# First units of a fused mLSTM and mixture-of-experts kernel: another order of the first loads, and a gate move in two transfers instead of three

## The chip, the cores and the metric

The kernel runs on one core of one Trainium2 chip. The metric is device time in microseconds, the median of several executions of the whole program.

## The reference

Four sequences of 768 steps with 8 heads of 40 go through a gated recurrence with a matrix memory; its output, 3072 tokens of 320, goes through a top-2 mixture of 8 experts. Cut to what matters:

```python
m_new  = np.maximum(f_gate[:, :, t] + m, i_gate[:, :, t])
f_stab = np.exp(f_gate[:, :, t] + m - m_new)
i_stab = np.exp(i_gate[:, :, t] - m_new)
C = f_stab * C + i_stab * outer(vt, kt)
n = f_stab * n + i_stab * kt
y[:, :, t] = sigmoid(o_gate) * (C @ qt) / np.maximum(abs(n @ qt), 1.0)
# then, on x = y as [3072, 320]:
noisy = x @ w_gate + noise * np.log1p(np.exp(x @ w_noise))
# top 2 of 8 experts, softmax over the two
out[mask] += top2_w * (np.maximum(x[mask] @ w1[e], 0) @ w2[e])
```

## The kernel before, in words

The recurrence is done in chunks of 64 steps. A **unit** is one chunk for one half of the batch (two sequences on the two partition halves, 8 heads); there are 24 units, 12 for each half. Four buffers rotate: unit u uses QK[u % 4] (queries and keys by feature) and VKS[u % 4] (values, keys by time, and the output gates). The mixture of experts follows in the second and longer part of the kernel, and its routing begins beside the units.

The schedule is manual: each engine works in the order in which the program issues instructions to it, and waits where an operand that another engine or a transfer writes isn't there. All loads of the first stretch go through SP's queue, in program order too; an issue that waits holds back the issues behind it.

What a unit does, by name:

- `load_unit(u, "k")` is two transfers of queries and keys (160 KB each, 40 partitions each) into QK; `load_unit(u, "v")` is two of 242 KB into VKS. Before a QK buffer is loaded its rows 32 to 63 and 96 to 127 are zeroed by `blank(i, engine)`.
- `gate_math` is eight VectorE instructions over 64 partitions that turn the gates of some steps (tile `raw`, loaded from `fi_in`, in several pieces) into the two rows of HL. `gate_move(kk)` carries the part of HL for two units into the operand tiles LE[kk % 2] and RE[kk % 2]: one transfer into LE (32 rows) and two into RE (row 96 and row 97, each gathered from 16 rows). Before unit 0, gate moves 0 and 1 go through SP's queue; later ones through GpSimd's queue, from iteration 13 on through SP's again.
- `operands` and `heads` fill the constant parts of LE and RE (ScalarE and VectorE).
- `e_part(u)` is one matmul for each half from LE and RE, and an exponential on ScalarE: the decay matrix W[u] (L308, L311).
- `s_part(u)` is the query-key products, 32 matmuls (L333), and for a unit that isn't a sequence's first, two longer ones per half with the identity `ident` as an operand (L329), which is in the first 128 columns of the constants `cs`.
- `k_part(u)` (VectorE, L341) multiplies `VKS[u % 4][:, :, 328:648]`, all 128 partitions of both halves, by a column of W[u], and gives KD[u]. `p_part(u)` (L347, L351 for a first unit) multiplies the products by W[u] and gives PP[u].
- `c_part(u)` (32 matmuls L361) forms the state from KD[u], and ScalarE copies it into VK[(u + 1) % 4] (L364). `o_part(u)` (32 matmuls L370) forms the output from PP[u]. `f_part` divides by the denominator and multiplies by the output gate (VectorE, then GpSimd L382).
- `keys(i)` prepares rows of VK[i] that no load writes: two zeroings (L244, L245) and two copies of `ident` (L246, L247), on GpSimd. Columns 328 to 648 of these rows lie in what `k_part` reads. In unit 0 `c_part` and `o_part` use only the loaded rows (`kr`).

Before the loop over units the program issues on TensorE: 16 warm-up matmuls on zeros (`WARM`), `s_part(0)`, 12 more (`WARM2`), `e_part(0)`, `s_part(1)`, `e_part(1)`. On VectorE behind the gate math of units 0 to 3 come `heads(1, 0)`, `k_part(0)`, `p_part(0)`, then `gate_math(256, 384)` and four further steps of gate math. Iteration i of the loop then has, on TensorE, `c_part(i)`, `o_part(i)`, half of `e_part(i+2)`, `s_part(i+2)`, the other half of `e_part(i+2)`; on VectorE `k_part(i+1)`, `p_part(i+1)`, `f_part(i)` and steps of gate math or routing; a gate move in every second iteration, two iterations ahead of its first use.

The order in which SP's queue gets the first loads is: gates of steps 0 to 127, constants `cet`, queries of unit 0, `ident`, gates 128 to 255, values of unit 0, gate move 0, queries and values of unit 1, gates 256 to 511, queries of unit 2, gate move 1, the rest of the gates, values of unit 2. GpSimd's is: `blank(1)`, `blank(2)`, `keys(0)`, `keys(1)`, `blank(3)`, `keys(2)`, `keys(3)`.

Of the kernel before, what the change touches and what calls it, by code (L numbers as in the profile page):

```python
# [7 lines left out]
F32 = mybir.dt.float32  # L8
# [28 lines left out]
NB = 4  # L37

STEP, SHARE = 0.19, 1.65
WARM, WARM2 = 16, 12  # L40
LEAD = 2
TURN = 6
OR1 = (0, 6, 1, 2, 3, 4, 5)
# [15 lines left out]
def build(ctx, tc, qk, vk, fi, noise, wgn, w1, w2, cst, ce, out):  # L59
    nc = tc.nc  # L60
    V, A, P, T, SP = nc.vector, nc.scalar, nc.gpsimd, nc.tensor, nc.sync
# [10 lines left out]
    cs = keep.tile([128, C_END], F32, name="cs")  # L72
# [24 lines left out]
    RE = [gates.tile([128, 2, H, GC * L], FR, name=f"re{i}") for i in range(2)]  # L97
# [53 lines left out]
    def load_unit(u, what="kv", q=None):  # L151
        pr, c = divmod(u, NCH)
        if "k" in what:
            for p in range(2):
                (q or SP).dma_start(QK[u % 4][64 * p:64 * p + D], qk[pr, c, p])
        if "v" in what:
            flat = VKS[u % 4].rearrange("p x c -> p (x c)")
            SP.dma_start(flat[0:64, 0:VW], vk[pr, c, 0])
            SP.dma_start(flat[64:128, 648:648 + VW], vk[pr, c, 1])
# [3 lines left out]
    fit = raw[0:64, 0:2 * S].rearrange("p (x t) -> p x t", x=2)  # L163
# [8 lines left out]
    def blank(i, q):  # L172
        q.memset(QK[i][32:64], 0.0)
        q.memset(QK[i][96:128], 0.0)
# [6 lines left out]
    V.memset(rmt[:, 0:256], 1.0)  # L181
    V.memset(rmt[:, 0:256].rearrange("p (c t) -> p c t", t=L)[:, :, 0], 0.0)
    load_unit(0, "k")
    SP.dma_start(cs[:, 0:128], cst[:, 0:128])
    SP.dma_start(fit[:, :, 128:256], fi[:, :, 128:256])
    load_unit(0, "v")

    def run(steps):
        for _ in steps:
            pass  # L190

    def gate_math(t0, t1):
        f, i = fit[:, 0, t0:t1], fit[:, 1, t0:t1]
        n = t1 - t0
        V.tensor_tensor_scan(mt[:, t0 + 1:t1 + 1], f, i, mt[:, t0:t0 + 1], OP.add, OP.max)
        yield
        gt = gts[t0 // 128 % 2][:, 0:n]
        V.tensor_add(gt, f, mt[:, t0:t1])
        yield
        V.tensor_sub(gt, gt, mt[:, t0 + 1:t1 + 1])  # L200
        if t0 == 0:
            V.memset(gt[:, 0:1], 0.0)
        yield
        ag = ags[t0 // 128 % 2][:, :, 0:n]
        V.tensor_tensor_scan(ag[:, 1, :], rmt[:, 0:n], gt, 0.0, OP.mult, OP.add)
        yield
        V.tensor_sub(ag[:, 0, :], i, mt[:, t0 + 1:t1 + 1])
        yield
        V.tensor_sub(ag[:, 0, :], ag[:, 0, :], ag[:, 1, :])
        yield  # L210

        V.tensor_copy(HL[:, :, t0:t1], ag)
        yield
        V.scalar_tensor_tensor(HL[:, :, t0:t1], HL[:, :, t0:t1].bitcast(F32), cet[0:64, E_SG:E_SG + 1], ag, op0=OP.mult, op1=OP.add)
        yield
# [3 lines left out]
    def gate_move(kk, q=(SP, SP)):  # L219
        pr, k = divmod(kk, GB)  # L220
        j = kk % 2
        src = HL[32 * pr:32 * pr + 32, :, k * GC * L:(k + 1) * GC * L].bitcast(F32)
        q[0].dma_start(LE[j][64:96, :, 64:128].bitcast(F32), src[:, 0].rearrange("r (c t) -> r c t", c=GC))
        for x in range(2):
            q[x].dma_start(RE[j][96 + x:97 + x].bitcast(F32), src[16 * x:16 * x + 16, 1])

    def operands(j, p, eng=None):
        if p is None:
            A.activation(LE[j][0:KE], cet[0:KE, None, E_L:E_L + 192].to_broadcast([KE, GC, 192]), AF.Copy)
        else:  # L230
            A.activation(RE[j][0:64, p].rearrange("r h (c t) -> r h c t", c=GC),
                         cet[0:64, None, None, 0:L].to_broadcast([64, H, GC, L]), AF.Copy)

    def heads(j, p, eng):
        o, i = RE[j][64:96, p], cet[64:96, E_H:E_H + H, None].to_broadcast([32, H, GC * L])
        x = cet[64:96, E_P + p:E_P + p + 1]
        if eng is A:
            A.activation(o, i, AF.Copy, scale=x)
        else:
            V.tensor_scalar(o, i, x, None, op0=OP.mult)  # L240


    def keys(i):
        P.memset(VK[i][1][32:64, 0:328], 0.0)  # L244
        P.memset(VK[i][0][96:128, 328:648], 0.0)  # L245
        P.tensor_copy(VK[i][0][64:104, 328:648].rearrange("p (h d) -> p h d", h=H), ident[64:104, None, 64:104].to_broadcast([40, H, D]))  # L246
        P.tensor_copy(VK[i][1][0:64, 328:648].rearrange("p (h d) -> p h d", h=H), ident[0:64, None, 0:D].to_broadcast([64, H, D]))  # L247

    operands(0, None, A)
    run(gate_math(0, GC * L))  # L250
    gate_move(0)
    operands(0, 0, A)
    operands(0, 1, A)
    heads(0, 0, A)
    heads(0, 1, V)
    load_unit(1, "k")
    load_unit(1, "v")
    SP.dma_start(fit[:, :, 256:512], fi[:, :, 256:512])
    blank(2, P)
    for i in range(2):  # L260
        keys(i)
    load_unit(2, "k")
    operands(1, None, A)
    operands(1, 0, A)
    operands(1, 1, A)
    run(gate_math(GC * L, 256))
    gate_move(1)
    blank(3, P)
    for i in range(2, 4):
        keys(i)  # L270
    SP.dma_start(fit[:, :, 512:], fi[:, :, 512:])
    load_unit(2, "v")
# [420 lines left out]
    p_part(0)  # L693
    run(gate_math(256, 384))
    gate_move(2, (P, P))
    gates2 = (s for t0 in (384, 512, 640) for s in gate_math(t0, t0 + 128))
    for _ in range(4):
# [87 lines left out]
    i = 0  # L785
    while i < NU - LEAD:
# [11 lines left out]
        if W1LD <= i < W1LD + 12 and i % 2 == 0:  # L798
            j = (i - W1LD) // 2
# [383 lines left out]
    with tc.If(over > 0):  # L1183
        for i in range(NE):
# [5 lines left out]
            x = xf[0:n, 0:RW]  # L1190
# [12 lines left out]
        with tc.If(most > BLK):  # L1203
            V.memset(ec, 0.0)
            with tc.For_i(0, NE, 1) as e:
                weights(e)
                with tc.For_i(0, NCH, 1) as c:
# [8 lines left out]
                    for r in range(2):  # L1216
                        x = xf[:, DM * r:DM * r + DM]
# [85 lines left out]
```

## Time and profile before

| what | value |
|---|---|
| median of three runs | 545.15 us (543.91, 545.15, 547.63) |
| the profiled execution's own time | 542.27 us |
| its span, first to last instruction | 540.5 us |
| mean granted TensorE clock | 0.969 of full |
| TensorE matmul busy | 519.2 us, 96% of the span |
| VectorE, ScalarE, GpSimd busy | 355.9, 249.3, 245.3 us |

The profiled execution lies 1.6 us under the fastest and 2.9 us under the median of the three runs; 1.77 us of its time lie outside its span. A term that is found in the trace is added to 542.27 us for that execution, and the same term to 545.15 us for the median.

### The profile page before, as it was taken

The numbers are of one execution on the slowest core, as the hardware profiler recorded it, in microseconds if no ns is written. First come the engines' busy times: TensorE is split into PE (matmuls) and PEld (weight loads), VectorE is DVE, ScalarE is ACT, GpSimd is POOL, SyncE is SP. The second block draws the span as 40 slices with busy tenths as digits, with TensorE's granted clock in tenths as the row PEclk, the third lists the DMA queues.
The fourth block names the chain that finished last, engine by engine and source line by source line (L and its number), as shares of the span: only waits on it lengthen the run. The fifth ranks groups of instructions, "written<-read, shape, count | busy, mean of one in ns | idle before, by whom it ended". The sixth has DMA issues, their size and how long they took to land.

```text
span 540.5 us, 13275 instructions
## 1 busy us (share of the span) xinstructions
PE 519.2 (96%) x5064; PEld 487.6 (90%) x5064; DVE 355.9 (66%) x956; ACT 249.3 (46%) x611; POOL 245.3 (45%) x329
## 2 busy tenths in 40 slices
PE   7999999998989999999999999999999999999992
PEld 3788888887988997899999999999999999999992
DVE  8898989999787558674675485467548537546310
ACT  7578877886532235441543254154326405515200
POOL 7446665545353674325705632570562345151042
PEclk9599999998987999999999999999999999999997
DMA  5889888689668265239518714941871583272032
GB/s 139 184 233 228 244 210 226 194 195 243 209 220 245 78 78 134 84 63 259 130 32 228 141 52 90 262 95 33 211 157 43 120 233 84 55 168 25 2 40 38
DMA packets 49990, 77.04 MB, mean 143 GB/s; under 512 B 10201, under 2 KB 39408, under 8 KB 49920
## 3 DMA queue, kind: packets, MB, share of 16 engines
q1 hardware_dynamic: 38848, 57.38, 38.4%
q0 software_dynamic: 11072, 18.74, 19.0%
q8 instruction: 42, 0.69, 0.5%
q14 instruction: 28, 0.23, 0.1%
HBM read 52.50 MB, written 17.48 MB: 129 GB/s over the span
## 4 chain that ended last, share of the span: by engine, by line
PE 82%; DVE 9%; DMA 3%; ACT 2%; issue 1%; POOL 1%; SPq 0%; POOLq 0%; DVEq 0%
PE s L956 22%; PE e L956 11%; PE o L983 5%; PE o L981 5%; PE o L982 5%; PE st L981 5%; PE st L983 5%; PE st L982 4%; PE s L333 4%; PE o L370 3%; PE e L308 3%; PE st L361 2%; PE xt L413 2%; DMA xg<-rows,tok 1%; PE xt L393 1%
## 5 line engine op out<-in xcount | busy, mean ns | idle before, releaser
L1007 POOL DMA_INDIRECT y_out<-y,tok x54 | 88.6, 1641 | 188.8 <-DVE y L997 185.9
L967 ACT ACTIVATE hh<-s 128x384 fp32r<-128x384 f32 (+3 forms) x91 | 42.6, 469 | 84.5 <-PE s L956 83.5
L956 PE MATMUL s<-xh,w1h 128*128 128x384 f32 (+6 forms) x273 | 77.5, 338 | 0.1
L744 POOL DMA_INDIRECT xg<-rows,tok x54 | 61.0, 1130 | 26.3 <-issue 14.9
L968 DVE SCALAR_TENSOR_TENSOR hlo<-s,hh 128x384 fp32r<-128x384 f32 (+3 forms) x91 | 47.5, 522 | 24.7 <-ACT hh L967 24.1
L956 PE MATMUL s<-xh,w1l 128*128 128x384 f32 (+6 forms) x273 | 61.9, 335 | 0.0
L983 PE MATMUL o<-w2h,hlo 128*128 128x320 f32 x192 | 59.1, 308 | 0.7 <-DVE hlo L968 0.7
L981 PE MATMUL o<-w2h,hh 128*128 128x320 f32 x192 | 59.4, 310 | 0.2 <-ACT hh L967 0.2
L982 PE MATMUL o<-w2l,hh 128*128 128x320 f32 x192 | 58.7, 306 | 0.0
L981 PE MATMUL st<-w2h,hh 128*128 128x320 f32 x168 | 51.9, 309 | 0.0
L983 PE MATMUL st<-w2h,hlo 128*128 128x320 f32 x168 | 51.6, 307 | 0.0
L982 PE MATMUL st<-w2l,hh 128*128 128x320 f32 x168 | 51.4, 306 | 0.0
L956 PEld LDWEIGHTS s<-xh,w1h 128*128 128x128 f32 x273 | 49.5, 189 | 1.6 <-ACT xh L776 0.4
L956 PEld LDWEIGHTS s<-xh,w1l 128*128 128x128 f32 x273 | 47.8, 188 | 1.0
L956 PE MATMUL s<-xl,w1h 128*128 128x384 f32 (+6 forms) x182 | 46.6, 337 | 0.2 <-DVE xl L777 0.2
L997 DVE TENSOR_SCALAR y<-o,gw 128x320 f32<-128x320 f32 x24 | 13.2, 550 | 43.1 <-PE o L983 43.1
L997 DVE TENSOR_SCALAR y<-st,gw 128x320 f32<-128x320 f32 x21 | 11.6, 550 | 43.3 <-PE st L983 43.3
L967 ACT ACTIVATE hh<-e 128x384 fp32r<-128x384 f32 (+3 forms) x45 | 21.2, 472 | 40.4 <-PE e L956 40.4
L382 POOL TENSOR_TENSOR xr<-tm,vk 128x320 f32<-128x320 f32 x24 | 21.0, 873 | 40.0 <-ACT lg L462 9.4
L956 PE MATMUL e<-xh,w1h 128*128 128x384 f32 (+6 forms) x135 | 38.9, 343 | 0.1
L983 PEld LDWEIGHTS o<-w2h,hlo 128*128 128x128 f32 x192 | 36.0, 188 | 0.9 <-DVE hlo L968 0.9
L981 PEld LDWEIGHTS o<-w2h,hh 128*128 128x128 f32 x192 | 36.0, 188 | 0.7 <-ACT hh L967 0.4
(233 smaller groups left out, 1325.3 us busy)
## 6 DMA issues: line engine op xcount, KB each, us to landing
vk<-vk_in SPq DMA_DIRECT2D x48, 242.0 KB
raw<-w_in SPq DMA_DIRECT2D x7, 1280.0 KB
qk<-qk_in SPq DMA_DIRECT2D x48, 160.0 KB
raw<-w_in SPq DMA_DIRECT2D x7, 1024.0 KB
y_out<-zrow SPq DMA_DIRECT2D x15, 320.0 KB
raw<-w_in SPq DMA_DIRECT2D x18, 256.0 KB
xt__2815<-xb SPq DMA_DIRECT2D x36, 72.0 KB
rows<-xr POOLq DMA_DIRECT2D x12, 160.0 KB, 5.5
```

The lines of the kernel that those rows point to most:

```text
L308: T.matmul(ps, LE[j][0:KE, c, 64 - 64 * p:192 - 64 * p], RE[j][0:KE, p, :, c * L:c * L + L], start=True, stop=True)
L333: T.matmul(SQ[u][:, p][half[p], h, :], q[r, 1, h, :], q[r, 0, h, :], start=True, stop=True)
L382: P.tensor_mul(XR[u], tm.rearrange("p h d -> p (h d)"), SG[u % 4])
L744: P.indirect_dma_start(out=XG[0:rows_of(e, t), t], out_offset=None, in_=XD[0:n], in_offset=bass.IndirectOffsetOnAxis(ap=token(e, t), axis= ...
L956: T.matmul(ps[:, 0:n], l, r, start=i == 0, stop=i == len(ops) - 1)
L967: A.activation(hi, x, AF.Relu)
L968: V.scalar_tensor_tensor(lo, x, 0.0, hi.bitcast(F32), op0=OP.max, op1=OP.subtract)
L981: T.matmul(ps, HH[:, j, c], W2H[:, j], start=j == 0, stop=False)
L982: T.matmul(ps, HH[:, j, c], W2L[:, j], start=False, stop=False)
L983: T.matmul(ps, HLO[:, j, c], W2H[:, j], start=False, stop=j == 7)
L997: V.tensor_scalar(y[0:n], ps[0:n], GW[e][0:n, t:t + 1], None, op0=OP.mult)
L1007: st = P.indirect_dma_start(out=out, out_offset=bass.IndirectOffsetOnAxis(ap=token(e, t), axis=0), in_=y[0:n], in_offset=None, compute_op= ...
```

## The change

The second unit's queries are loaded ahead of gate move 0, right behind the second piece of the gates. `ident` and the values of unit 0 are issued behind gate move 0, the values of unit 1 behind those. Gate move 1 comes ahead of the queries of unit 2 and of the gates 256 to 511. A gate move's two transfers into RE become one, from 32 rows into rows 96 and 97, on the second queue of the pair. `keys` is split into its zeroings (`no_keys`) and its copies (`keys`), and the buffers are prepared in the order 1, 2, 3, 0: both zeroings of 1 and 2, the copies of 1 and 2, `blank(3)`, and then zeroings and copies of 3 and of 0. The second warm-up falls from 12 matmuls to 8.

```diff
-WARM, WARM2 = 16, 12
+WARM, WARM2 = 16, 8
@@
     load_unit(0, "k")
-    SP.dma_start(cs[:, 0:128], cst[:, 0:128])
     SP.dma_start(fit[:, :, 128:256], fi[:, :, 128:256])
-    load_unit(0, "v")
+    load_unit(1, "k")
@@ gate_move
-        for x in range(2):
-            q[x].dma_start(RE[j][96 + x:97 + x].bitcast(F32), src[16 * x:16 * x + 16, 1])
+        q[1].dma_start(RE[j][96:98].bitcast(F32), src[:, 1])
@@
-    def keys(i):
+    def no_keys(i):
         P.memset(VK[i][1][32:64, 0:328], 0.0)
         P.memset(VK[i][0][96:128, 328:648], 0.0)
+
+    def keys(i):
         P.tensor_copy(VK[i][0][64:104, 328:648]...)
         P.tensor_copy(VK[i][1][0:64, 328:648]...)
@@
     gate_move(0)
+    SP.dma_start(cs[:, 0:128], cst[:, 0:128])
+    load_unit(0, "v")
     operands(0, 0, A)
     operands(0, 1, A)
     heads(0, 0, A)
     heads(0, 1, V)
-    load_unit(1, "k")
     load_unit(1, "v")
-    SP.dma_start(fit[:, :, 256:512], fi[:, :, 256:512])
     blank(2, P)
-    for i in range(2):
+    for i in (1, 2):
+        no_keys(i)
+    for i in (1, 2):
         keys(i)
-    load_unit(2, "k")
     operands(1, None, A)
     operands(1, 0, A)
     operands(1, 1, A)
     run(gate_math(GC * L, 256))
     gate_move(1)
+    load_unit(2, "k")
+    SP.dma_start(fit[:, :, 256:512], fi[:, :, 256:512])
     blank(3, P)
-    for i in range(2, 4):
+    for i in (3, 0):
+        no_keys(i)
         keys(i)
```

## Rows read from the trace of the kernel before

**Rows 1.** The page: busy tenths of TensorE and the granted TensorE clock in 40 slices of 13.5 us.

```profile
PE   7999999998989999999999999999999999999992
PEclk9599999998987999999999999999999999999997
```

**Rows 2.** The chain of work that ended last, its first 45 us, in order of time: start in us, duration in us, what.

```profile
8.22 2.70 PE o L680 x12
...
10.92 0.24 PE e L308
...
14.21 4.55 DMA re<-hl
...
18.90 0.77 PE e L308
...
22.79 1.25 PE st L361 x32
24.05 1.71 PE o L370 x32
...
29.72 0.75 PE st L361 x32
30.47 0.93 PE o L370 x32
...
34.57 0.75 PE st L361 x32
...
39.42 0.75 PE st L361 x32
...
41.10 0.43 PE e L308
```

**Rows 3.** The waits of TensorE between 10 and 30 us: total in us, times, longest.

```profile
PE s L329 <- DMA qk<-qk_in: 1.8, 1, 1.8
PE e L308 <- DMA re<-hl: 0.9, 1, 0.9
```

**Rows 4.** Short stretches of time: busy time of each engine in the stretch, then the granted clock (PEclk), the share of the DMA engines and GB/s as the last three columns.

```profile
9.00:9.50 0.50, 0.50 (x4) 0.23 (x3) 0.47 (x3) 0.50 (x1) 0.41 (x2) 1.00 0.09 17
...
15.00:15.20 0.20, 0.20 (x2) 0.00 (x0) 0.00 (x0) 0.14 (x1) 0.18 (x1) 0.68 0.72 179
15.20:15.40 0.20, 0.20 (x6) 0.16 (x6) 0.00 (x0) 0.20 (x1) 0.17 (x1) 0.50 1.00 246
...
28.60:28.80 0.20, 0.20 (x9) 0.20 (x4) 0.17 (x2) 0.20 (x1) 0.20 (x1) 0.69 0.95 297
```

**Rows 5.** The timeline of the first 30 us, SP's queue: start in us, duration of the issue, line, target and source. Where one row merges issues, their count stands at its end.

```profile
1.49 0.61 SPq L177 DMA_DIRECT2D raw<-ce_in  x1
...
3.85 0.37 SPq L184 DMA_DIRECT2D cs<-cst_in  x1
...
7.02 0.73 SPq L223 DMA_DIRECT2D le<-hl  x1
...
7.79 1.22 SPq L225 DMA_DIRECT2D re<-hl  x2
...
11.21 0.60 SPq L258 DMA_DIRECT2D raw<-fi_in  x1
```

**Rows 6.** The same timeline, GpSimd and one row of ScalarE: the number in brackets is idle time before the row and what ended it.

```profile
2.74 0.94 POOL L173 MEMSET qk<- 32x1024 f32 x1
...
3.85 0.52 ACT L229 ACTIVATE le<-raw 98x384 fp32r<-98x384 f32 x1 [1.83 <-DMA raw<-ce_in]
...
4.73 0.36 POOL L244 MEMSET vk<- 32x328 f32 x1
...
7.27 0.75 POOL L246 COPY vk<-cs 40x320 f32<-40x320 f32 x1 [1.78 <-DMA cs<-cst_in]
...
8.06 0.48 POOL L247 COPY vk<-cs 64x320 f32<-64x320 f32 x1
...
12.98 0.36 POOL L244 MEMSET vk<- 32x328 f32 x1
...
13.82 0.45 POOL L246 COPY vk<-cs 40x320 f32<-40x320 f32 x1
...
14.82 0.36 POOL L244 MEMSET vk<- 32x328 f32 x1
```

**Rows 7.** The same timeline, VectorE and one row of TensorE.

```profile
12.36 0.82 DVE L341 TENSOR_TENSOR kd<-vk,w 128x640 f32<-128x640 f32 x1 [0.33 <-issue]
13.10 1.40 DVE L351 TENSOR_TENSOR p<-s,w 64x512 f32<-64x512 f32 x2
...
13.20 0.65 PE L329 MATMUL s<-qk,cs 64*64 64x512 f32 x2 [1.83 <-DMA qk<-qk_in]
...
16.31 0.57 DVE L195 TENSOR_TENSOR_SCAN xg<-raw,xg 64x128 f32<-64x128 f32 x1 [1.81 <-DMA raw<-fi_in]
...
20.71 0.79 DVE L341 TENSOR_TENSOR kd<-vk,w 128x640 f32<-128x640 f32 x1
21.54 1.23 DVE L347 TENSOR_TENSOR p<-s,w 128x1024 f32<-128x1024 f32 x1
```

**Rows 8.** The tile `re` between 30 and 130 us: from the issue of a transfer to its landing, over the 18 transfers; and one pair of issues from GpSimd's queue in the timeline.

```profile
30.79 0.98 POOL L225 DMA_DIRECT2D re<-hl  x2
...
DMA to landing us min/median/max: 4.5/6.2/8.2
```

## The prediction

> **What bounds the kernel now.** I read the page first. TensorE is busy in nearly every slice, and only one slice of the early stretch, the second, runs at the lower of its two clock levels (1.2 instead of 2.4 GHz) [rows 1]. A gain or loss in the first units therefore passes to the end almost whole, as long as TensorE is what the units wait for: from unit 3 on one unit takes 4.85 us (34.57 to 39.42), with TensorE's pieces end to end in the chain [rows 2].
>
> Next the chain of its first 30 us, and the waits in it. The second warm-up ends at 10.92 us and the first decay matmuls follow at once. Then TensorE stands for 1.8 us until unit 1's queries land, and later 0.9 us until gate move 1 lands, at about 18.8 us; the chain runs through that transfer [rows 2, 3]. The short stretches show the clock: full until 15.1 us, half until 28.7 us, full from there [rows 4]. The fall comes after the stand for the queries. A unit in the slow stretch took 6.93 us (22.79 to 29.72) against 4.85 us [rows 2], so the slow clock costs some 2.1 us in each unit that it covers. These two stands and the slow clock are what the change can win back, and the slow clock is the larger part.
>
> **The change part by part.** *Unit 1's queries sooner* takes away the 1.8 us stand: they are issued ahead of gate move 0, that is before 7.02 us [rows 5], not behind it. What is late next for the same products is `ident`, which now lies behind gate move 0. SP still waits there for the gate math, so the move into LE starts at 7.02 us, the move into RE at 7.79 us, and with one issue of 0.61 us (half of 1.22) instead of two, `ident` is issued at 8.42 us instead of 3.85 us [rows 5]. How long it then takes is bounded by two rows. `cet`, with little ahead of it, took from 1.49 us to 3.85 us, 2.4 us; `ident` itself, behind unit 0's queries, took from 3.85 us to 7.27 us, 3.4 us [rows 5, 6]. At 9 us the queues were moving only 17 GB/s [rows 4], so I take the lower one: `ident` lands at about 10.8 us (10.8 to 11.8). The products of unit 1 can start at about 11 us instead of 13.2 [rows 7].
>
> *Four warm-up matmuls fewer* are 4 x 0.225 us (2.70 over 12), 0.9 us [rows 2]. *Gate move 0* is issued complete 0.6 us sooner. The two belong together, and the first decay matmuls move forward by at most 0.9 us; all of this disappears in the wait that follows.
>
> *The copies for buffer 0 last* is where I think the change loses. `k_part(0)` reads columns 328 to 648 of all 128 partitions of VKS[0], and half of these rows are written by `keys(0)`. That it makes no use of them in unit 0 doesn't help: VectorE has to wait for GpSimd. Before, `keys(0)` was the first of four and was over at 8.5 us, and `k_part(0)` started at 12.36 us without waiting for it [rows 6, 7]. Now it is the last of four, and GpSimd's queue stands at the copies of buffer 1 until `ident` lands. What is behind that landing on GpSimd:
>
> - four pairs of copies at 1.00 us (13.82 to 14.82), 4.0 us [rows 6];
> - `blank(3)`, 1.99 us where VectorE was not in its way (2.74 to 4.73) [rows 6];
> - zeroings of buffers 3 and 0, two pairs at 0.84 us (12.98 to 13.82), 1.7 us [rows 6].
>
> That is 7.7 us behind 10.8 us: `k_part(0)` starts at 18.5 us instead of 12.36 us, 6.1 us later. The bounds are 18.3 us and, with the later landing and half a microsecond of disturbance on GpSimd, 20.0 us. The zeroings of buffers 1 and 2, which move ahead of the landing, take 1.7 us from 4.73 us and hide there.
>
> Queued behind `k_part(0)` on VectorE are `p_part(0)`, the gate math of the next two units and `k_part(1)`; TensorE waits for both products. KD[0] is there at 19.4 us (0.82 us), PP[0] at 20.8 us (1.40 us) [rows 7]. TensorE, done with its decay matmuls at about 13 us, stands for more than 6 us, and its clock will be at the lower level, as it was in the trace after a stand of 1.8 us. `o_part(0)` runs from 20.8 us for 1.71 us [rows 2], to 22.5 us. Then comes the decay matmul that had started at 18.90 us [rows 2]: 3.6 us late.
>
> *Gate move 1 sooner* is worth the 0.9 us in that place [rows 3], and this gain is already in the 3.6: the transfer, issued from 11.3 us, behind the four issues of values of units 0 and 1, has until 22.5 us, so its landing, 4.55 us from the last issue before [rows 2], is covered. If the cover is gone (the first rival), it is what counts.
>
> *The gates 256 to 511* are issued at about 13.5 us (gate move 1 in 1.3 us, unit 2's queries in 0.9) instead of 11.21 us. Before, they landed 5.1 us after their issue (16.31) and VectorE stood 1.8 us for them [rows 5, 7]; by the same time they land at 18.6 us, ahead of 20.8 us: hidden. From there VectorE needs 4.4 us to `k_part(1)` (16.31 to 20.71) [rows 7], so KD[1] is there at 26.0 us and PP[1] at 27.3 us. TensorE, 3.6 us late, comes to them at 26.4 and 27.7 us. VectorE is just in time and adds nothing.
>
> *The clock.* If it rises at the same place in the work, the whole 3.6 us stay. If it rises at the same moment, 28.7 us, then 3.6 us of work that ran at half speed before run at full speed, and 1.8 us stay. I see no row that decides and take the middle, **2.7 us slower**.
>
> *Gate moves in two transfers*: each saves 0.49 us of GpSimd (half of 0.98) or 0.61 us of SP [rows 5, 8], both off the chain in the units. In return one transfer gathers 32 rows into two instead of 16 into one. The landing is 4.5 to 8.2 us; the first use of the move issued at 30.79 us comes at 41.10 us, 10.3 us later [rows 2, 8]. So 2.1 us are free even behind the slowest: I cost it at nothing, with no gain below that either, since no decay matmul in the units waited for one.
>
> The Trainium skill, page "DMA: Bandwidth & Descriptors", section "Why a DMA increments its semaphore by 16 and not by 1", says that a transfer is spread over the largest number of DMA engines, up to 16, that divides the slowest dimension of both its sides. By that a transfer into two rows goes over two engines, with 16 pieces of 512 bytes on each. No row here shows how many engines a transfer used. It speaks against this part of the change, and is taken up as the third rival.
>
> The sum: 542.27 + 2.7 = 545.0 us for an execution like the profiled one. The median lies 2.9 us above that one, and the same term on it gives 545.15 + 2.7 = 547.8 us.
>
> **The rivals.** *First, `k_part(0)` is not held* (the wait isn't made, or GpSimd gets there much sooner). Then its operand that comes last is the values of unit 0, issued until 10.1 us (two issues of some 0.6 us behind `ident`'s) and landed at about 12.5 us by the 2.4 us above; TensorE goes from unit 1's decay matmuls into `c_part(0)` at 13.4 us with no long stand, and the clock may stay up. The bound is then VectorE, which stands for the later gates: 18.6 us (17.5 if they land a microsecond sooner), 4.4 us, and `k_part(1)`, `p_part(1)` 2.0 us, so that `o_part(1)` starts at 24 to 25 us against 24.05 us [rows 2, 7]. What is left is the clock behind it: 0.8 us in `o_part(1)` (1.71 against 0.93) [rows 2] and about as much in unit 3's products. 1.7 us faster, 543.4 us. For it speaks that unit 0's own matmuls don't use the copied rows; against it that the instruction reads them.
>
> *Second, the low clock lasts.* The stand of 6 us is longer than any in the units, and if the clock rises one or two units later than I assume, at 2.1 us each, the loss is 5 to 7 us: 551 us. For it speaks that VectorE is only just in time for units 1 and 2, so TensorE may have small stands while it should be recovering; against it that TensorE's work behind 22.5 us is the same as before 28.7 us.
>
> *Third, the one transfer into RE lands late,* in every second unit. It decides from 10.3 us between issue and landing, 2.1 us above the slowest before [rows 8]. One microsecond beyond that in each of ten moves is 10 us: 555 us. Against it: 16 pieces more in a row would have to cost 0.13 us each before the slack behind the slowest is gone. The spread over two engines, by the page named above, would push this way.
>
> **How the numbers follow.** My forecast has 0.68, the first rival 0.15, the second 0.10, the third 0.05. 0.02 is left for a start without stands on any engine, which would win back most of the slow clock: three units at 2.1 us, over 5.4 us. One per cent is 5.4 us, about what a measurement of this kernel can tell from no change. The forecast (1.8 to 3.6 us, to 5 us with the later landing of `ident`) and the first rival lie within it; the second lies half beyond, the third beyond. So faster has 0.03, slower 0.09, the rest is the same: 0.88. The range reaches from the first rival's time to the second's: 543.2 to 551.0 us. It covers a microsecond or so by which three runs of one kernel shift their median.
>
> **What would show it.** Right: in the changed trace the first `kd` instruction waits for GpSimd's copy into `vk` and starts at 18 to 20 us; TensorE stands for about 6 us ahead of the first `st` matmuls, and no longer for `qk`; the second landing wait, for `re`, is gone; the chain runs through GpSimd's copies; `st` of unit 3, at 34.57 us before, starts 2 to 4 us later. Wrong: `kd` at 12 to 13 us, or a clock that stays full through 30 us, would leave the loss without a cause; waits of `e` matmuls for `re` in the units would say that the third rival has come in. If the copies of `ident` start well behind 11 us, the loss is larger by as much.

## The result and the profile after

The changed kernel is slower: 1.008 of the time before, with a 95% interval of 1.0052 to 1.0108. On 545.15 us that is 4.4 us (2.8 to 5.9). The medians of 20 runs each are 550.37 and 547.81 us; they hold executions with a disturbed clock, which the ratios here leave out, and of the profiles of e2 and e4 below, which are such executions, only the start is read (40 us, and 140 us for e4's waits). I had forecast 2.7 us more, 547.8 us, and had given 0.88 to "no more than one per cent either way". The point lies inside that band, but the loss is clear of no change and larger than I made it.

The chain that ended last in the changed kernel, first 40 us (start, duration, what), answers to [rows 2]:

```profile
8.61 1.87 DMA cs<-cst_in
...
10.62 0.45 POOL vk L246
...
18.15 0.45 POOL vk L247
...
19.34 4.76 DMA vk<-vk_in
...
24.14 0.48 ACT vk L320
...
25.12 0.78 DVE kd L345
...
28.14 1.94 PE o L374 x32
...
33.59 0.75 PE st L365 x32
...
38.44 0.75 PE st L365 x32
```

Up to 18.6 us it runs where the prediction had put it: the transfer of `ident`, then GpSimd's four pairs of copies. Between there and TensorE it names a load of unit 3's values and ScalarE's work on output gates, and then VectorE's `kd` of unit 1. That `kd` reads neither. In its own timeline VectorE stands nowhere between 18.63 and 28 us, so I read this stretch as VectorE's and these two names as bystanders. The state matmuls (`st`) of unit 3 start at 38.44 us instead of 34.57 us, 3.87 us late, and those of unit 2 are late by the same 3.87 us (33.59 against 29.72). The waits of the first 40 us (total, times, longest) answer to [rows 3]:

```profile
DVE kd L345 <- DMA raw<-fi_in: 7.0, 1, 7.0
...
PE st L365 <- DVE kd L345: 6.5, 1, 6.5
...
POOL vk L246 <- DMA cs<-cst_in: 4.3, 1, 4.3
```

TensorE no longer stands for `qk` or `re`; it stands 6.5 us for the first `kd`. That `kd` waits 7.0 us, and the row names a transfer of gates, which `kd` doesn't read. It landed at about the moment at which the last copy ended; the first experiment shows that both are there. A second trace of the same kernel (e11 below) puts the same stand to the copy:

```profile
18.59 0.83 DVE L345 TENSOR_TENSOR kd<-vk,w 128x640 f32<-128x640 f32 x1 [7.02 <-POOL vk L247]
```

VectorE's timeline of the first trace answers to [rows 7]; the last number in brackets is idle time and what ended it:

```profile
18.63 0.83 DVE L345 TENSOR_TENSOR kd<-vk,w 128x640 f32<-128x640 f32 x1 [7.02 <-DMA raw<-fi_in]
...
25.11 0.79 DVE L345 TENSOR_TENSOR kd<-vk,w 128x640 f32<-128x640 f32 x1
25.93 1.22 DVE L351 TENSOR_TENSOR p<-s,w 128x1024 f32<-128x1024 f32 x1
...
27.51 0.49 DVE L385 SCALAR_TENSOR_TENSOR tm<-dn,o 128x320 f32<-128x320 f32 x1
```

And TensorE's output matmuls of unit 1:

```profile
28.14 1.94 PE L374 MATMUL o<-vk,p 104*64 104x41 f32 x32 [0.28 <-DVE tm L385]
```

`kd` of unit 0 is 6.3 us late, and `kd` of unit 1 is 4.4 us late (25.11 against 20.71 in [rows 7]): the 1.8 us that VectorE stood for gates before are used up, the rest stays. Unit 1's output matmuls stand 0.28 us for `tm`, the end of unit 0's `f_part`, because there is one buffer for `o`.

The granted clock (third column from the right) fell and rose here, answering to [rows 4]:

```profile
15.00:15.20 0.20, 0.00 (x0) 0.00 (x0) 0.00 (x0) 0.00 (x0) 0.20 (x1) 0.65 0.84 169
...
32.00:32.20 0.20, 0.20 (x12) 0.20 (x8) 0.17 (x2) 0.20 (x1) 0.00 (x0) 0.68 1.04 399
```

The span of this execution is 547.4 us, 6.9 us over the 540.5 us before. Of this, 3.9 us lie in the first 34 us. Of the rest, 2.4 us are four stands of TensorE in front of `st` matmuls between 95 and 130 us that the profile puts to nothing; the second trace of the same kernel has a span of 540.9 us, and the second one of the kernel before has 542.1 us, the other way round. So I read single traces for where the engines wait and the ratios for how much.

### The profile page after: what moved, and what is told of

Its sections match the earlier page's. It is cut to its first block, busy times and chain, and to the rows that moved or that the text cites. A ratio compares the mean times of both kernels' runs of the same rounds, so it can differ in the third digit from the quotient of the medians.

```text
span 547.4 us, 13223 instructions
## 1 busy us (share of the span) xinstructions
PE 518.1 (95%) x5059; PEld 486.6 (89%) x5060; DVE 352.7 (64%) x956; ACT 249.5 (46%) x611; POOL 242.9 (44%) x322
## 3 DMA queue, kind: packets, MB, share of 16 engines
q0 software_dynamic: 10960, 18.74, 18.9%
## 4 chain that ended last, share of the span: by engine, by line
PE 79%; DVE 6%; DMA 5%; ACT 3%; POOL 2%; issue 2%; another core or an unknown queue 1%; SPq 1%; POOLq 0%; DVEq 0%
PE s L960 21%; PE e L960 11%; PE o L987 5%; PE o L985 5%; PE o L986 5%; PE st L985 4%; PE st L987 4%; PE st L986 4%; PE o L374 4%; PE s L337 4%; PE e L312 3%; PE st L365 3%; PE xt L417 2%; DMA qk<-qk_in 2%; PE xt L397 1%
```

## The experiments

All ratios are to the kernel before, measured beside it on the same chip. The table has for each run the start of `kd` of unit 0, of `kd` of unit 1, and of `st` of unit 3 in the timeline, in us.

| kernel | kd 0 | kd 1 | st 3 | ratio (95%) |
|---|---|---|---|---|
| before; second trace | 12.36; 12.60 | 20.71; 20.68 | 34.50; 35.64 | 1 |
| changed; second trace | 18.63; 18.59 | 25.11; 25.08 | 38.37; 37.27 | 1.008 (1.0052 to 1.0108) |
| e1 half the rows | 12.74, 13.79 | 23.05 | 36.84 | 1.0015 (0.9967 to 1.0062) |
| e2 copies 0 to 3 | 13.58 | 22.67 | 36.44 | 1.0052 (1.0012 to 1.0091) |
| e3 before, copies last | 16.65 | 23.13 | 35.35 | 1.0054 (1.0025 to 1.0083) |
| e4 before, one move | 12.42 | 19.95 | 32.98 | 1.0015 (0.9982 to 1.0047) |
| e6 changed, warm | 18.60 | 25.08 | 38.71 | 1.0118 (1.0005 to 1.0231) |
| e7 half, gates early | 13.38, 14.43 | 21.32 | 34.78 | 1.0101 (0.9984 to 1.0219) |
| e10 the same again | 13.40, 14.44 | 21.31 | 34.77 | 0.9999 (0.9953 to 1.0045) |
| e8 first attempt | 13.66 | 19.38 | 33.94 | 0.9995 (0.9932 to 1.0059) |
| e9 second attempt | 12.69 | 18.47 | 32.00 | 1.0031 (0.9981 to 1.0081) |

**Is it the copies?** In e1 unit 0's `k_part` reads only the rows that it uses:

```diff
+            for p in range(0 if u else 2):
+                n = half[p]
+                V.tensor_mul(KD[u][n, p], VKS[u % 4][n, p, 328:648]..., W[u][n, p, :, L - 1:L]...)
+            if not u:
+                return
             V.tensor_mul(KD[u], VKS[u % 4][:, :, 328:648]..., W[u][:, :, :, L - 1:L]...)
```

> The changed kernel, but unit 0's state product reads only the half of the rows that it uses (two instructions of 64 partitions in place of one of 128), so that it needs none of the copies into buffer 0; GpSimd's order stays. Theory (the wait for the copies costs 3.9 us): the first kd starts when the values of unit 0 land, at 12.5 to 13 us instead of 18.63 us, the first st matmul at about 13.5 us instead of 19.51 us; then VectorE stands for the gates 256 to 511 until at most 18.6 us, so that the st of unit 3, at 38.37 us in the changed kernel and 34.50 us before, comes at 33 to 34.5 us, and the time is 0 to 1.7 us under the kernel before (ratio 0.997 to 1.000). Rival (the wait is for the gates landing, which the profile names for the 7.0 us in front of the first kd): kd still starts at 18.6 us and the ratio stays near 1.008.

VectorE's timeline of e1:

```profile
12.74 0.48 DVE L347 TENSOR_TENSOR kd<-vk,w 64x320 f32<-64x320 f32 x1 [1.18 <-DMA vk<-vk_in]
13.79 0.49 DVE L347 TENSOR_TENSOR kd<-vk,w 64x320 f32<-64x320 f32 x1 [0.56 <-ACT w L315]
14.31 1.41 DVE L361 TENSOR_TENSOR p<-s,w 64x512 f32<-64x512 f32 x2
18.74 0.48 DVE L194 TENSOR_TENSOR_SCAN xg<-raw,xg 64x128 f32<-64x128 f32 x1 [3.02 <-DMA raw<-fi_in]
...
23.05 0.79 DVE L351 TENSOR_TENSOR kd<-vk,w 128x640 f32<-128x640 f32 x1
```

`kd` moves from 18.63 to 12.74 us with nothing changed but the rows it reads, in two pieces: the copies held it, not the transfer that the wait's row names. But the transfer is there too. Now VectorE stands 3.0 us for the gates, until 18.74 us, and `kd` of unit 1 comes only 2.1 us sooner than in the changed kernel. The start gets back 1.5 us of the 3.9, not all of it as I had expected; the ratio, 1.0015, is above the 0.997 to 1.000 that I had expected, and its interval reaches from a gain to most of the loss.

e2 keeps the whole instruction and puts the copies back in the order 0, 1, 2, 3:

```diff
-    for i in (1, 2):
+    for i in (0, 1):
         no_keys(i)
-    for i in (1, 2):
+    for i in (0, 1):
         keys(i)
@@
-    for i in (3, 0):
+    for i in (2, 3):
```

> The changed kernel with the buffers prepared in the order 0, 1, 2, 3 again; loads, warm-up and gate moves as changed. Theory: ident lands at 10.5 us as in the changed kernel, the copies into buffer 0 are over at about 11.9 us, and kd is held only by the values of unit 0, as when it reads half the rows: kd at 12.5 to 13 us, the st of unit 3 at 33 to 34.5 us, ratio 0.997 to 1.000. Rival (the later landing of ident or of the gates is what costs): st of unit 3 stays at 37 to 38.4 us, ratio 1.005 to 1.008.

The start is that of e1: `kd` at 13.58 us, held by the values of unit 0, unit 1's at 22.67 us, `st` of unit 3 at 36.44 us. I had expected 33 to 34.5 us, and was wrong in the same way: with the copies out of the way the later gates hold VectorE, which the rival of this run had as its cause. The ratio, 1.0052, is clear of no change.

**The copies alone.** e3 changes nothing else in the kernel before:

```diff
-    for i in range(2):
+    for i in (1, 2):
         keys(i)
@@
-    for i in range(2, 4):
+    for i in (3, 0):
         keys(i)
```

> The kernel before, with the buffers prepared in the order 1, 2, 3, 0 and nothing else. Theory: ident lands at 7.3 us as before, GpSimd's four pairs of copies end where they ended before, at 16.6 us, so kd of unit 0 starts at 16.7 us instead of 12.36 us; PP of unit 0 is there at 18.9 us, its output is done at 20.6 us, and the decay matmul that stood until 18.9 us comes at 20.6 us: the st of unit 3 at 36.2 us instead of 34.50 us (plus 1.7 us, 0.2 us either way), ratio 1.003. Rival (the order of the copies is innocent, the loads cost): st of unit 3 at 34.5 us, ratio 1.000.

VectorE and GpSimd in e3:

```profile
16.17 0.45 POOL L247 COPY vk<-cs 64x320 f32<-64x320 f32 x1
...
16.65 0.82 DVE L341 TENSOR_TENSOR kd<-vk,w 128x640 f32<-128x640 f32 x1 [4.62 <-POOL vk L247]
```

The wait is to the point: `kd` at 16.65 us (16.7 expected), right behind the last copy, and here the row names it. The kernel is slower by 1.0054 (1.0025 to 1.0083), more than the 1.003 expected though with it in the interval. The `st` of unit 3 was a miss: 35.35 us, not 36.2 us, which is between the two traces of the kernel before (34.50 and 35.64), so this loss is shown by the ratio and not by the start of one trace. By the ratio the order of the copies alone makes a large part of the loss. What the loads alone make is what e1 and e2 leave, 0.8 to 2.8 us by their ratios, of which only e2's is clear of no change. In the changed kernel the two lie beside one another: each holds VectorE until some 18.6 us, and taking one away leaves the other. (In e3 the copies end at 16.6 us: the later landing of `ident` moves them the other 2 us.)

**Without both.** e7, and e10 the same kernel measured again, is e1 with the gates 256 to 511 right behind `ident`:

```diff
     SP.dma_start(cs[:, 0:128], cst[:, 0:128])
+    SP.dma_start(fit[:, :, 256:512], fi[:, :, 256:512])
     load_unit(0, "v")
@@
     load_unit(2, "k")
-    SP.dma_start(fit[:, :, 256:512], fi[:, :, 256:512])
```

> The changed kernel with unit 0's state product on half of the rows, and the gates 256 to 511 issued right behind ident instead of behind the queries of unit 2. Theory (what is left of the loss when kd no longer waits is VectorE's stand for these gates): they land by 12.5 us, VectorE doesn't stand for them, kd of unit 1 starts at 20.3 us instead of 23.05 us, the st of unit 3 at 34 to 34.5 us instead of 36.84 us, ratio 0.996 to 1.000. Rival (the low clock holds the units, not VectorE): st of unit 3 at 36 us or later.

> The changed kernel without both waits (unit 0's state product on half of the rows, gates 256 to 511 right behind ident) once more, since its time was left open (interval 0.998 to 1.022). Theory (the two waits lie beside one another and are the whole loss): st of unit 3 at 34 to 35.5 us, ratio 0.997 to 1.002. Rival (something later in the changed kernel costs too, the single transfer into RE or the order of the later loads): ratio 1.005 or more.

VectorE in e10:

```profile
14.96 1.41 DVE L361 TENSOR_TENSOR p<-s,w 64x512 f32<-64x512 f32 x2
16.39 0.62 DVE L194 TENSOR_TENSOR_SCAN xg<-raw,xg 64x128 f32<-64x128 f32 x1
...
21.31 0.79 DVE L351 TENSOR_TENSOR kd<-vk,w 128x640 f32<-128x640 f32 x1
```

The scan follows the product with no stand in between; `kd` of unit 1 is 1 us later than I had expected (the values of unit 0 land 0.7 us later behind the gates), and `st` of unit 3 comes at 34.77 us, between the two traces of the kernel before. The ratio is 0.9999 (0.9953 to 1.0045); e7 had left it open at 1.0101 from three runs. Weighted by their intervals the two give about 1.001 (0.997 to 1.006), less than the 1.008 of the changed kernel. The two waits account for the loss as far as this can be measured: nothing later in the changed kernel needs to be added, but up to 3 us of something else would not show.

**The single move alone.** e4 has only the two transfers into RE as one.

> The kernel before, with the two transfers into RE as one and nothing else. Theory (worth nothing in the units): no decay matmul between 30 and 130 us waits for re; gate move 1 lands 0 to 0.5 us sooner, since its last issue ends half a microsecond sooner; ratio 0.999 to 1.001. Rival (the one transfer lands later because its pieces lie on fewer queues): the decay matmul at 18.9 us comes at 19.5 us or later, and decay matmuls in the units wait for re; up to 1 us in each of ten moves, ratio up to 1.018.

The decay matmul of unit 2 starts at 18.41 us instead of 18.90 us, its wait for `re` still there:

```profile
PE e L307 <- DMA re<-hl: 2.2, 1, 2.2
```

That is half a microsecond sooner, as expected, and it is the only wait for `re` up to 140 us. Its `st` of unit 3, 32.98 us, is 1.5 us ahead of the first trace of the kernel before, with the low clock lying elsewhere (19.7 to 26.5 us); the ratio shows no gain. For the landing, the second trace of the changed kernel has, on the tile `re` up to 130 us:

```profile
L223 POOL DMA_DIRECT2D re<-hl x7: 632/637/691, 25.2 to 84.5; - x7
...
DMA to landing us min/median/max: 3.4/4.8/6.1
```

The issue of 0.64 us replaces two of 0.49 us, and the landing is no slower than the 4.5, 6.2 and 8.2 us of [rows 8] (over the stretch of those rows, 30 to 130 us, it is 4.8, 4.8 and 6.1 us). The page "DMA: Bandwidth & Descriptors" of the Trainium skill (section "Why a DMA increments its semaphore by 16 and not by 1") would spread this transfer over fewer engines; no run shows the number, and no longer landing is to be seen.

**The clock.** The kernel before and the changed one, each traced once more without an edit:

> The kernel before, looked at once more. If the low stretch of TensorE's clock belongs to the schedule, it falls at 15.1 us and rises at 28.7 us again and the st of unit 3 comes at 34.5 us. If its moments differ from one execution to the next (in the two kernels closest to this one it fell at 17.8 and 19.7 us and rose at 27.7 and 26.5 us), the st of unit 3 comes up to 1.5 us sooner, at 33.0 us, and a difference of one or two microseconds between two single looks at the start is the clock's, not the schedule's.

> The changed kernel, looked at once more. Theory (the start is held by VectorE, which the clock doesn't touch): kd of unit 0 at 18.6 us, kd of unit 1 at 25.1 us, unit 1's output matmuls not before 28.1 us, and the st of unit 3 at 37.5 to 39 us, with the low clock wherever it lies; the units behind lose no more than in the kernel before.

In the kernel before the low stretch lasted from 14.2 to 31.2 us this time (15.1 to 28.7 in [rows 4]), and `st` of unit 3 came at 35.64 us, 1.1 us later: its moments differ between executions of one kernel, and the other way from what I had guessed. In the changed kernel it lasted from 16.0 to 29.7 us (15.1 to 32.1), with VectorE's instructions within 0.05 us of the first trace up to 30 us, and `st` of unit 3 at 37.27 us, a little below what I had expected. So the 3.9 us between the two first traces are 1.6 us between the second ones, and 2.7 and 2.8 us crosswise: about 1 us either way moves with the clock.

e6 fills TensorE's stand in the changed kernel:

```diff
     e_part(1, first=True)
+    warm(28)
     k_part(0)
```

> The changed kernel with 28 more warm-up matmuls (6 us) behind unit 1's decay matmuls, in the stand of TensorE. Theory (of the 3.9 us a part is the low clock): the clock stays full through the stand, kd stays at 18.6 us and the first st at 19.5 us, units 0 and 1 run at full clock up to where VectorE holds them (kd of unit 1 at 25.1 us, its product at 27.2 us), and the st of unit 3 comes at 36 to 36.5 us instead of 38.37 us; ratio to the kernel before 1.002 to 1.005. Rival (the clock costs nothing here, VectorE holds everything): st of unit 3 at 38 us, ratio 1.008.

TensorE in short stretches in e6:

```profile
13.00:19.00 6.00, 6.00 (x29) 2.56 (x27) 0.40 (x1) 1.17 (x3) 5.26 (x12) 1.00 0.92 219
19.00:26.00 7.00, 4.45 (x104) 3.48 (x104) 6.59 (x17) 4.34 (x10) 1.48 (x2) 1.00 0.82 176
26.00:26.40 0.40, 0.40 (x12) 0.40 (x14) 0.40 (x1) 0.33 (x1) 0.00 (x0) 0.53 0.41 138
26.40:32.00 5.60, 4.88 (x78) 4.16 (x78) 5.39 (x12) 2.03 (x5) 1.49 (x2) 0.50 0.33 105
```

The clock stayed full through the stand and unit 0, but TensorE won nothing: from 19 to 26 us VectorE is busy for 6.59 of 7.00 us, and unit 1's output matmuls start at 28.11 us (28.14 without the fill), again when `tm` is there. The clock then fell at 26.0 us, after a stand of 1.8 us in front of unit 1's `st`, and stayed low to 32.9 us. `st` of unit 3 comes at 38.71 us, and the ratio, 1.0118 (1.0005 to 1.0231) from three runs, is nearer the rival's numbers than mine, with mine inside its interval. Up to 28.1 us VectorE sets the start of the changed kernel. What a full clock would give back behind that e6 doesn't show, since it was low there; in the second trace, where it rose at 29.7 instead of 32.1 us, `st` of unit 3 came 1.1 us sooner.

**Two attempts at a version that beats both.** e8 takes e7 but leaves `ident` and the values of unit 0 ahead of gate move 0, and moves the four early steps of gate math one iteration on:

```diff
     load_unit(1, "k")
+    SP.dma_start(cs[:, 0:128], cst[:, 0:128])
+    load_unit(0, "v")
@@
     gate_move(0)
-    SP.dma_start(cs[:, 0:128], cst[:, 0:128])
-    load_unit(0, "v")
+    SP.dma_start(fit[:, :, 256:512], fi[:, :, 256:512])
@@
-    for _ in range(4):
-        next(gates2)
@@
-        if i < 5:
+        if i < 6:
```

> A version meant to beat both: unit 1's queries first, ident and the values of unit 0 still ahead of gate move 0, the gates 256 to 511 right behind it, one transfer into RE, unit 0's state product on half of the rows, and the four early steps of gate math one iteration later. Theory: kd of unit 0 at 12 us, kd of unit 1 at 18 to 19 us, the st of unit 3 at 31.5 to 33 us, 1.5 to 3 us ahead of the kernel before; ratio 0.994 to 0.998. Rival (the low clock and the landing of unit 2's queries hold it): st of unit 3 at 34 us, ratio 1.000.

Its decay matmuls of unit 0 wait for gate move 0:

```profile
12.52 0.47 PE L312 MATMUL e<-re,le 98*128 98x512 f32 x1 [2.63 <-DMA re<-hl]
```

With unit 1's queries and unit 0's values both ahead of it, gate move 0 lands at 12.5 us, where the changed kernel started these matmuls at 10.32 us. So, with unit 1's queries ahead of gate move 0, the values of unit 0 belong behind it: that is worth 2.2 us in this place. In the kernel before, with the values ahead and the queries behind, no wait stood here [rows 2, 3]. The `st` of unit 3 comes at 33.94 us, not at 31.5 to 33 us as expected: the rival's 34 us. e9 therefore keeps the values behind, only `ident` ahead, and adds 8 warm-up matmuls behind unit 1's decay matmuls; its decay matmuls of unit 0 start at 10.34 us.

> A second version meant to beat both, after the first let gate move 0 land late (12.5 us) behind the values of unit 0. The changed order of loads, with ident ahead of gate move 0 and the values of unit 0 and then the gates 256 to 511 right behind it; unit 0's state product on half of the rows; the four early steps of gate math one iteration later; 8 warm-up matmuls more behind unit 1's decay matmuls. Theory (three waits and the low clock set the start): decay matmuls of unit 0 at 10.3 us, kd of unit 0 at 12.5 to 13 us, kd of unit 1 at 18 to 19 us, st of unit 3 at 29 to 31 us with the clock full, ratio 0.990 to 0.995. Rival (the clock falls all the same, at 15 to 20 us, and TensorE at half speed holds the units): st of unit 3 at 32 to 33 us, ratio 0.996 to 0.999.

The `st` matmuls of units 1 to 5 in e9:

```profile
20.43 0.82 PE L371 MATMUL st<-vk,kd 104*40 104x41 f32 x32
26.05 0.82 PE L371 MATMUL st<-vk,kd 104*40 104x41 f32 x32
32.00 0.82 PE L371 MATMUL st<-vk,kd 104*40 104x41 f32 x32
38.38 0.82 PE L371 MATMUL st<-vk,kd 104*40 104x41 f32 x32
46.43 1.32 PE L371 MATMUL st<-vk,kd 104*40 104x41 f32 x32
```

Unit 2 is 3.6 us ahead of the kernel before (26.05 against 29.65), the clock full. Unit 3 comes at 32.00 us, not at 29 to 31 us; that is the rival's time but not its cause, since the clock stayed full. Unit 5 is 2.2 us behind the kernel before (46.43 against 44.20). Between units 2 and 5 the chain has these pieces:

```profile
20.07 8.65 DMA re<-hl
...
33.34 1.28 issue
...
40.56 2.50 issue
```

Gate move 2 took 8.65 us to land and TensorE stood 1.1 us for it; then it stood 1.28 and 2.50 us for nothing that the profile shows, and the clock fell behind the second of these, at 45.3 us. The ratio is 1.0031 (0.9981 to 1.0081). Why TensorE stood there stays open, and neither attempt beats the kernel before.

## Why the prediction was right or wrong

**Right:** the mechanism, its place and its time. `ident` issued at 8.42 us and landed at 10.8 us in the forecast; 8.61 and 10.5 to 10.6 us in the trace. `kd` of unit 0 at 18.5 us; 18.63 us. The decay matmul behind unit 0's output at 22.5 us; 22.69 us. The gates landing at 18.6 us; at 18.7 us where e1 lays them bare. The single move is worth nothing in the units, and the stands for `qk` and `re` are gone.

**Wrong: the last term of the sum, 2.7 us;** the runs have 4.4 us (2.8 to 5.9). The step that failed is what the clock gives back: out of a delay of 3.6 us I took off 0.9 us, the middle between nothing and 1.8 us, without a row for it. In the chains unit 1's output starts 4.1 us late in the first pair of traces (28.14 against 24.05 [rows 2]) and 3.8 us late in the second (28.11 against 24.35). So the delay was 0.2 to 0.5 us short. A part of that is that VectorE is not "just in time": I had left out `f_part(0)`, which comes behind PP[1] on VectorE and has to clear the one `o` buffer, and TensorE stood 0.28 us for it. Behind 28.1 us the clock gave back 0.2 us in the first pair (3.9 us left at `st` of unit 3) and 2.2 us in the second (1.6 us left), so something like each of my two ends occurs. The ratio, from many more runs, is at the whole delay with nothing given back; its interval leaves room for 1.3 us. That the mean over both traces of each kernel, 2.75 us, is the forecast is luck, with traces of one kernel 1.1 us apart. Why the ratio has more than this mean stays open. Two numbers of the forecast have no working: the lower bound of 18.3 us for `kd`, and the lower end of the range, 543.2 us, where the first rival's time is 543.4 us.

By VectorE's own rows the term is 4.4 us (25.11 less 20.71), which is what the ratio gives; that they agree to the tenth is chance, since the clock moves a single trace by about 1 us. e6, with the clock full to 26.0 us, shows that a faster TensorE gains nothing before VectorE is done at 28 us; it is no test of what lies behind.

**The chances.** I had called one per cent, 5.4 us, about what a measurement here can tell from no change, and on that "the same" got 0.88. This failed too: the interval is 1.5 us either way, and the case that took 0.88 had no word for a loss that is under one per cent and yet clear of no change. The interval reaches over 5.4 us, so whether the 0.09 for a larger loss was too low isn't settled.

**The first rival** was mis-sized too: without the wait for the copies the kernel is not 1.7 us faster than before but, by the ratios of e1 and e2, 0.8 and 2.8 us slower; e2's interval excludes a gain, e1's just reaches 1.8 us. I had VectorE's stand for the gates right, and `kd` of unit 1 at about 23 us (18.6 plus 4.4), but let the clock stay up; it fell at 17.5 us in e1. **The second rival** (the low clock lasts) isn't shown: the low stretch lasted 17.0 and 13.7 us in the two traces of the changed kernel, and 13.6 and 17.0 us in those of the kernel before. **The third** didn't come in.

## What to carry to other kernels

Follow a reordered preparation to every instruction that reads its bytes, not to the unit that uses its values: a full-width instruction made VectorE wait for copies that its own unit never needed. When one wait on an engine is removed or added, list what else on that engine's queue is late at about the same time (here copies and gates, both at 18.6 us), since only the later of the two counts, and include the work that frees single buffers. A lead won in the first units need not last: of e9's 3.6 us, 1.1 us went into a stand for a transfer and more into stands whose cause the profile doesn't show.

## What the runs showed of the hardware

The low stretch of TensorE's clock at the start doesn't belong to the schedule alone: two traces of one kernel had it from 15.1 to 28.7 us and from 14.2 to 31.2 us, and two kernels nearly the same had it later and shorter (17.6 to 27.8 us in e3, 19.7 to 26.5 us in e4). With it `st` of unit 3 moves by 1.1 us in either kernel (34.50 and 35.64, 38.37 and 37.27 us), which is a good part of the effects looked for; in e4, where it came at 32.98 us, half a microsecond is the single move's, and how much of the rest is the clock's isn't shown. And the wait that a row names can be a bystander: 7.0 us were put to a transfer that the instruction doesn't read, when it landed about as the true cause ended, and a second trace of the same kernel put the same 7.0 us to the true cause, GpSimd's copy.
